# Talking-heads attention and two gated layers on one core: values fetched before the relayouts, fewer clock-keeping matmuls, chunk rows 12 partitions apart, q in its own pool

## The chip, the cores and the metric

The kernel runs on one NeuronCore of a Trainium2 chip. The metric is the device time of one execution in microseconds (us); lower is better. The engines are TensorE (PE, with its weight loads listed as PEld), VectorE (DVE), ScalarE (ACT), GpSimd (POOL) and SyncE (SP). SP, POOL and ACT also issue DMAs; a row of the trace that names such an issue writes the engine as SPq or ACTq.

## The reference

Twelve heads of attention for two batches of 448 positions, with the heads mixed by a 12x12 matrix before the softmax and by another after it, and then two gated layers:

```python
scores = scale * np.matmul(q, k.transpose(0, 1, 3, 2))
scores = np.einsum('bhij,hg->bgij', scores, w_pre)
scores = scores - np.max(scores, axis=-1, keepdims=True)
attn = np.exp(scores)
attn = attn / (np.sum(attn, axis=-1, keepdims=True) + 1e-09)
attn = np.einsum('bhij,hg->bgij', attn, w_post)
out = np.matmul(attn, v)
x = out.transpose(0, 2, 1, 3).reshape(B * S, H * D)          # 896 x 768
x = (silu(x @ w_gate) * (x @ w_val)) @ w_out                 # hidden 1536
y = ((h := x @ w_in) * clip(h + 3, 0, 6) / 6) @ w_out2       # hidden 2048
```

The matrices of the two layers arrive in 64-bit floating point and are turned into pairs of 32-bit parts on the chip.

## The kernel before, in words

**Tiles and chunks.** The 448 query positions of a batch are cut into four tiles (TILES, L34), eight tiles in all, numbered t = 0 to 7. A tile is cut into chunks of ten query rows (KI): the eight tiles have 10, 12, 12, 11, 12, 12, 11 and 10 chunks, 90 in all. Two chunks make a pair, and the main loop takes one pair per step, i = 0 to 44, with two lead-in steps before.

**Scores.** `scores(t, c)` (L152) multiplies q by k for head pair c into two PSUM banks, and `scores_out` (L175) copies them, one head on DVE and one on ACT, into the tile's score buffer S: query rows on the partitions, 13 slots of 448 on the free axis (12 heads and a zero slot). There are two score buffers (L136), so tile t+2 overwrites what tile t held.

**Relayouts.** The mix over heads needs the heads on partitions. `relayout(m)` (L184) takes the ten query rows of chunk m out of S. In the kernel before they stand `ncc` partitions apart (ncc is the tile's number of chunks: 10, 11 or 12). SP sends the first eight rows (8 x 13 slots) to partitions 0 to 103 of a tile sx, and `relayout_rest` (L199) sends the other two rows from POOL to partitions 104 to 127; this POOL transfer is called the rest below. sx holds a pair and has six buffers.

**One step.** In program order step i holds: the exponentials of pair i+1 on ACT; the product of attention and values, `av` (L283) and `av_rest` (L305), of an earlier tile; `postmix(i)` (L253), the mix after the softmax; the softmax weights of pair i+1 on DVE; the copy of the mixed weights; `premix(i+2)` (L208), which reads sx, and its row maxima on DVE; and the scores of a later tile. Attention times values begins in step 5; it needs four pieces of v, which `load_v(0, 0)` to `load_v(0, 3)` fetch in steps 0 to 3. The last piece is read by `av_rest` alone, just ahead of `postmix(5)`.

**Queues.** The order is written out by hand: extra work is hung on steps with `at_step`, at named places within a step, and each engine works its list in order. So does SP, which issues nearly all transfers: q, k, v, the relayouts and the weights of the layers. S is read by the relayouts of a tile until the last of them has landed; only then may the scores of the tile after next be copied into that buffer.

**Clock.** `keep_clock` (L489) issues matmuls on a tile of zeros whose result nobody reads: 7 at the start and 17 after the scores of the first two tiles, ahead of the first premix.

**The layers.** After step 44 come the last products with values, then the two gated layers with their weights streamed in (L411).

Of the kernel before, what the change touches and what calls it, by code (L numbers as in the profile page):

```python
# [7 lines left out]
F32 = mybir.dt.float32  # L8
# [15 lines left out]
KG = 5  # L24
KI = 2 * KG
# [8 lines left out]
TILES = [  # L34
    [(0, 100, 10), (100, 120, 12), (220, 120, 12), (340, 108, 11)],
    [(0, 120, 12), (120, 120, 12), (240, 110, 11), (350, 98, 10)],
]
SQ = 45 * KI

WARM = (7, 17)  # L40

LOOK = 2

# [4 lines left out]
def kernel(  # L48
# [14 lines left out]
    nc = tc.nc  # L63
# [20 lines left out]
    big = ctx.enter_context(tc.tile_pool(name="big", bufs=4, side="right"))  # L84
# [9 lines left out]

    qs, ks, vs = {}, {}, {}

    def new_qk(b):
        qs[b] = big.tile([128, HP * SQ], F32, name=f"q{b}", tag="big")
        ks[b] = big.tile([128, HP, S], F32, name=f"k{b}", tag="big")

    def load_q(b, i0, i1):
        lo, hi = (HP * KI * sum(c for _, _, c in TILES[b][:i]) for i in (i0, i1))
        nc.sync.dma_start(out=qs[b][:, lo:hi], in_=qT[b, :, lo:hi])

    def load_k(b, c0, c1, eng=nc.sync):
# [10 lines left out]
    def load_q0(c0, c1, eng):
        n = TILES[0][0][2] * KI
        eng.dma_start(out=qs[0][:, c0 * n : c1 * n], in_=qT[0, :, c0 * n : c1 * n])

    new_qk(0)  # L120
    load_q0(0, 2, nc.sync)
# [9 lines left out]
    nc.scalar.dma_start(out=W1, in_=w_pre)  # L131
    nc.scalar.dma_start(out=W2.rearrange("p g k -> p (g k)"), in_=w_post)
    nc.gpsimd.tensor_scalar(W1, W1, 0.125, 1.0, ALU.mult, ALU.mult)
    load_q(0, 1, 2)

    Ss = [psc.tile([128, H + 1, S], F32, name=f"S{i}") for i in range(2)]  # L136
    for x in Ss:
# [12 lines left out]
    stiles, pqk = {}, {}  # L150

    def scores(t, c, tags=("pqk", "pqk")):  # L152

        b, i = divmod(t, 4)
        n = TILES[b][i][2] * KI
        if c == 0:
            stiles[t] = Ss[t % 2]
        base = HP * KI * sum(x for _, _, x in TILES[b][:i]) + c * n
        p = [bank(f"pqk{t}_{c}_{e}", tags[e]) for e in range(2)]
        for s in range(2):  # L160
            lo, hi = 64 * s, min(64 * s + 64, n)
            for e in range(2):
                r = slice(64 * e, 64 * e + 64)
                nc.tensor.matmul(  # L164
                    p[e][lo:hi, :S],
                    lhsT=qs[b][r, base + lo : base + hi],
                    rhs=ks[b][r, c, :],
                    start=True,
                    stop=True,
                    tile_position=(64 * e, 64 * s),  # L170
                )
        for e in range(2):
            pqk[t, 2 * c + e] = p[e]

    def scores_out(t, c):  # L175
        n = TILES[t // 4][t % 4][2] * KI
        for e in range(2):
            h = 2 * c + e
            copy = nc.scalar.copy if e else nc.vector.tensor_copy
            copy(stiles[t][:n, h, :], pqk.pop((t, h))[:n, :S])  # L180

    sx = {}

    def relayout(m):  # L184

        t, c = chunks[m]  # L190
        b, i = divmod(t, 4)
        ncc = TILES[b][i][2]
        i, r = divmod(m, 2)
        if r == 0:
            sx[i] = psx.tile([128, 2, S], F32, name=f"sx{i}", tag="sx")
        rows = stiles[t][c : ncc * KI : ncc, :, :]
        nc.sync.dma_start(out=sx[i][0:104, r, :], in_=rows[:8, :, :])

    def relayout_rest(m):  # L199
        t, c = chunks[m]  # L200
        b, i = divmod(t, 4)
        ncc = TILES[b][i][2]
        rows = stiles[t][c : ncc * KI : ncc, :, :]
        nc.gpsimd.dma_start(out=sx[m // 2][104:128, m % 2, :], in_=rows[8:, :H, :])  # L204

    pre, tot, ew, wns, post, ats = {}, {}, {}, {}, {}, {}

# [281 lines left out]
    def keep_clock(n):  # L489

        p = ps.tile([128, 512], F32, name=f"clock{n}", tag="ppost", bufs=BUFS["ppost"])
        for _ in range(n):
            nc.tensor.matmul(p[:, :480], lhsT=idle[:, :128], rhs=idle, start=True, stop=True)

    keep_clock(WARM[0])
    placed = 0
    for t in range(2):
        for c in range(HP):
            scores(t, c, (("pqk", "pqk"), ("ppre", "ppre"), ("ppost", "ppost"), ("ppre", "pav"))[(6 * t + c) % 4])
            scores_out(t, c)  # L500
        if t == 0:
            load_q(0, 2, 3)
            for _ in range(8):
                relayout(placed)
                relayout_rest(placed)
                placed += 1
    keep_clock(WARM[1])
    rests = placed
    new_v(0)


    extra = {i: {"qk0": [], "S0": [], "av2": [], "out2": [], "qk": [], "av": [], "S": [], "rest0": [], "rest1": [], "out": [], "end": []} for i in range(-LOOK, NP)}
# [1 line left out]
    def at_step(i, f, *args, place="end"):  # L514
        extra[i][place].append((f, args))
# [272 lines left out]
```

## Time and profile before

| | us |
|---|---|
| median of 3 runs | 702.42 (701.99 to 703.91) |
| the profiled execution, its own time | 702.33 |
| its span in the trace | 700.5 |
| PE busy in the span | 678.0 (97%) |
| DVE busy | 504.3 (72%) |
| ACT busy | 297.6 (42%) |

The profile page gives busy time, 40 slices of the span and the chain of work that ended last. Its span runs from the first to the last instruction; the execution's own time is 1.83 us longer. A matmul that waits inside its pipeline counts as busy, so 97% is not 97% of the peak.

### The profile page before, as it was taken

How to read it: one execution, taken by the hardware profiler on the slowest of the kernel's cores; microseconds unless marked ns; L12 is line 12 of the kernel's file. 1: busy time of each engine (PE TensorE's matmuls, PEld its weight loads, DVE VectorE, ACT ScalarE, POOL GpSimd, SP SyncE). 2: the span in 40 equal slices, each digit the busy share in tenths (PEclk: the TensorE clock that was granted, in tenths of full speed). 3: DMA queues.
4: the chain of work that ended last, by engine and by line, in shares of the span. 5: the costliest groups of instructions: out<-in, count | busy, mean ns of one | idle time of the engine just before them, and what ended most of it. 6: DMA issues, size and time to landing. Idle time of an engine off the chain costs nothing.

```text
span 700.5 us, 16097 instructions
## 1 busy us (share of the span) xinstructions
PE 678.0 (97%) x6696; PEld 567.5 (81%) x6696; DVE 504.3 (72%) x836; ACT 297.6 (42%) x603; POOL 147.9 (21%) x179
## 2 busy tenths in 40 slices
PE   9769998999899999999999999999999999999998
PEld 3336565666589999999999999999999999999997
DVE  4447779988718888888888656668888888665550
ACT  4435676777623433334333323334455444332320
POOL 2413234542601112111211000004323422000000
PEclk9978999999999999999999999999999999999999
DMA  5574676555502433333324332232233223444420
GB/s 180 176 216 133 174 201 201 165 144 142 162 3 90 134 97 130 95 133 117 109 91 131 112 119 91 94 131 91 90 99 127 91 83 121 146 148 147 144 66 26
DMA packets 34200, 86.69 MB, mean 124 GB/s; under 512 B 9328, under 2 KB 22016, under 8 KB 34128
## 3 DMA queue, kind: packets, MB, share of 16 engines
q1 hardware_dynamic: 26208, 81.01, 36.3%
q0 software_dynamic: 7200, 3.94, 2.4%
q8 instruction: 52, 0.85, 0.5%
q10 hardware_dynamic: 720, 0.73, 0.3%
q14 instruction: 20, 0.16, 0.1%
HBM read 62.20 MB, written 2.75 MB: 93 GB/s over the span
## 4 chain that ended last, share of the span: by engine, by line
PE 87%; DMA 4%; DVE 4%; issue 2%; ACT 2%; SPq 1%; POOL 0%; ACTq 0%; POOLq 0%
PE pi L411 17%; PE pp L411 17%; PE po L411 12%; PE pv L411 11%; PE pg L411 11%; PE ppre L215 4%; PE pqk L164 4%; PE pav L291 4%; PE ppost L261 3%; DMA sx<-S 3%; PE p L411 2%; PE pav L311 2%; DMA v<-in_v_dram 2%; ACT e L236 1%; DVE nm L228 1%
## 5 line engine op out<-in xcount | busy, mean ns | idle before, releaser
L411 PE MATMUL pp<-g,hp 128*128 128x448 f32 x384 | 109.1, 365 | 0.0
L411 PE MATMUL po<-u,ho 128*128 128x448 f32 x288 | 81.7, 364 | 0.0
L652 POOL TENSOR_TENSOR g<-rl,g 128x448 fp32r<-128x448 f32 x32 | 41.7, 1323 | 169.1 <-ACT g L651 169.1
L411 PEld LDWEIGHTS pp<-g,hp 128*128 128x128 f32 x384 | 71.9, 187 | 5.8
L204 POOL DMA_DIRECT2D sx<-S x90 | 52.1, 579 | 105.3 <-issue 25.9
L236 ACT ACTIVATE e<-ppre,nm 128x448 f32<-128x448 f32 x90 | 56.3, 631 | 39.0 <-DVE nm L228 38.9
L411 PE MATMUL pi<-x2h,li 128*128 128x448 f32 x192 | 70.2, 366 | 0.0
L411 PE MATMUL pi<-x2l,hi 128*128 128x448 f32 x192 | 70.0, 364 | 0.0
L411 PE MATMUL pi<-x2h,hi 128*128 128x448 f32 x192 | 69.9, 364 | 0.0
L411 PE MATMUL pp<-g,lp 128*128 128x448 f32 x192 | 69.3, 361 | 0.0
L652 POOL TENSOR_TENSOR u<-sg,u 128x448 fp32r<-128x448 f32 x24 | 32.7, 1382 | 154.1 <-ACT u L651 154.1
L291 PEld LDWEIGHTS pav<-at,v 128*64 128x64 f32 x576 | 28.6, 138 | 36.3 <-ACT xs L334 18.3
L228 DVE TENSOR_REDUCE nm<-ppre 128x1 f32<-128x448 f32 x90 | 51.9, 617 | 7.2 <-PE ppre L215 4.9
L411 PEld LDWEIGHTS po<-u,ho 128*128 128x128 f32 x288 | 54.1, 188 | 3.8
L215 PE MATMUL ppre<-sx,W 64*64 64x448 f32 x360 | 52.9, 555 | 3.2 <-DMA sx<-S 2.8
L261 PE MATMUL ppost<-wn,e 60*64 60x60 f32 x2520 | 53.5, 224 | 1.3 <-issue 0.6
L411 PE MATMUL po<-u,lo 128*128 128x448 f32 x144 | 52.3, 363 | 0.0
L261 PEld LDWEIGHTS ppost<-wn,e 60*64 60x64 f32 x2520 | 47.0, 137 | 4.8 <-ACT at L279 1.7
L164 PE MATMUL pqk<-k,q 64*64 64x448 f32 (+3 forms) x384 | 50.7, 567 | 0.0
L411 PE MATMUL pg<-xl,hg 128*128 128x448 f32 x132 | 48.3, 366 | 0.0
L411 PE MATMUL pv<-xl,hv 128*128 128x448 f32 x132 | 48.3, 366 | 0.0
L411 PE MATMUL pg<-xh,hg 128*128 128x448 f32 x132 | 48.2, 365 | 0.0
(97 smaller groups left out, 1401.4 us busy)
## 6 DMA issues: line engine op xcount, KB each, us to landing
sx<-S SPq DMA_DIRECT2D x90, 182.0 KB
ri<-in_moe_w_in_dram SPq DMA_DIRECT2D x16, 768.0 KB
ro<-in_moe_w_out_dram SPq DMA_DIRECT2D x12, 768.0 KB
rg<-in_moe_w_gate_dram SPq DMA_DIRECT2D x11, 768.0 KB
rv<-in_moe_w_val_dram SPq DMA_DIRECT2D x11, 768.0 KB
rp<-in_moe_w_out_dram SPq DMA_DIRECT2D x12, 640.0 KB
rp<-in_moe_w_out_dram SPq DMA_DIRECT2D x6, 768.0 KB
sx<-S POOLq DMA_DIRECT2D x90, 42.0 KB, 5.4
```

Of the source, the lines that this page charges most:

```text
L164: nc.tensor.matmul(p[e][lo:hi, :S], lhsT=qs[b][r, base + lo : base + hi], rhs=ks[b][r, c, :], start=True, stop=True, tile_position=(64 * e ...
L204: nc.gpsimd.dma_start(out=sx[m // 2][104:128, m % 2, :], in_=rows[8:, :H, :])
L215: nc.tensor.matmul(p[a][64 * r : 64 * r + 64, :S], lhsT=W1[rows, :], rhs=x[rows, r, :], start=True, stop=True, tile_position=(64 * a, 64 * r),
L228: nc.vector.tensor_reduce(nm[:, a : a + 1], pre[i][a][:, :S], AX.X, ALU.max, negate=True)
L236: nc.scalar.activation(e2[a], p[a][:, :S], AF.Exp, bias=nm[:, a : a + 1], scale=1.0, accum_out=sm[:, a : a + 1])
L261: nc.tensor.matmul(p[s][64 * c : 64 * c + 64, at, :, :], lhsT=e2[a][rows, 64 * k : 64 * k + 64], rhs=wn[rows, a, :].rearrange("p (g k) -> ...
L291: nc.tensor.matmul(p[64 * e : 64 * e + 64, : 2 * n], lhsT=vs[b][:, jc, h, :], rhs=ats[t][:, 2 * jc : 2 * jc + 2, h, :n], start=jc == 0, st ...
L311: mm = nc.tensor.matmul(pavs[t, c][64 * e : 64 * e + 64, a * n : a * n + n], lhsT=vs[b][rows, JC - 1, h, :], rhs=ats[t][rows, KB - 1, h, : ...
L411: nc.tensor.matmul(p[:, :S], lhsT=wt[:, kk, :], rhs=xx, start=start, stop=stop)
L652: eng.tensor_tensor(to[1], src, to[0].bitcast(F32), ALU.subtract)
```

## The change

It does five things.

1. q no longer lies in one big buffer per batch. Each tile has its own q tile in a rotating pool of three buffers, and a batch's `big` buffers now hold k alone.
2. The rows of a chunk in S are always 12 partitions apart (STRIDE), whatever the tile's number of chunks. The tiles with 10 and 11 chunks get padding rows in q, so their score buffers fill 118 or 119 partitions where they filled 100 or 110.
3. The first two pieces of v are loaded ahead of the first relayouts; the q of tile 2 goes to SP behind the first eight relayouts.
4. The second run of clock-keeping matmuls has 6 for 17.
5. One early group of scores, (2, 3) in step 4, uses the bank `pav` for one of its two results, where it used `pqk` for both.

```diff
-SQ = 45 * KI
+STRIDE = 12
+ROWS = [[STRIDE * (KI - 1) + n for _, _, n in t] for t in TILES]
-WARM = (7, 17)
+WARM = (7, 6)
...
+    pq = left.enter_context(tc.tile_pool(name="pq", bufs=3, side="left"))
...
-    def new_qk(b):
-        qs[b] = big.tile([128, HP * SQ], F32, name=f"q{b}", tag="big")
+    def new_k(b):
         ks[b] = big.tile([128, HP, S], F32, name=f"k{b}", tag="big")
-    def load_q(b, i0, i1):
-        lo, hi = (HP * KI * sum(c for _, _, c in TILES[b][:i]) for i in (i0, i1))
-        nc.sync.dma_start(out=qs[b][:, lo:hi], in_=qT[b, :, lo:hi])
+    def load_q(t, c0=0, c1=HP, eng=nc.sync):
+        b, i = divmod(t, 4)
+        n = ROWS[b][i]
+        if c0 == 0:
+            qs[t] = pq.tile([128, HP * STRIDE * KI], F32, name=f"q{t}", tag="q")
+        base = HP * sum(ROWS[b][:i])
+        eng.dma_start(out=qs[t][:, c0 * n : c1 * n], in_=qT[b, :, base + c0 * n : base + c1 * n])
...
-    load_q(0, 1, 2)
+    load_q(1)
+    new_v(0)
+    for j in range(2):
+        load_v(0, j)
...
-        n = TILES[b][i][2] * KI
+        n = ROWS[b][i]
...
-        rows = stiles[t][c : ncc * KI : ncc, :, :]
-        nc.sync.dma_start(out=sx[i][0:104, r, :], in_=rows[:8, :, :])
+        rows = stiles[t][c : c + 7 * STRIDE + 1 : STRIDE, :, :]
+        nc.sync.dma_start(out=sx[i][0:104, r, :], in_=rows)
...
-        rows = stiles[t][c : ncc * KI : ncc, :, :]
-        nc.gpsimd.dma_start(out=sx[m // 2][104:128, m % 2, :], in_=rows[8:, :H, :])
+        rows = stiles[t][c + 8 * STRIDE : c + 9 * STRIDE + 1 : STRIDE, :H, :]
+        nc.gpsimd.dma_start(out=sx[m // 2][104:128, m % 2, :], in_=rows)
...
         if t == 0:
-            load_q(0, 2, 3)
             for _ in range(8):
                 relayout(placed)
                 relayout_rest(placed)
                 placed += 1
     keep_clock(WARM[1])
+    load_q(2)
     rests = placed
-    new_v(0)
...
             if t == 2 and c == 3:
-                at_step(4, scores, t, c, place="qk0")
+                at_step(4, scores, t, c, ("pav", "pqk"), place="qk0")
...
-    loads = [(j, load_v, 0, j) for j in (0, 1, 2, 3)] + [(2, load_q, 0, 3, 4), (5, load_q, 1, 0, 1)]
+    loads = [(j - 2, load_v, 0, j) for j in (2, 3)] + [(2, load_q, 3), (5, load_q, 4)]
-    loads += [(13, load_q, 1, 1, 2), (19, load_q, 1, 2, 3), (25, load_q, 1, 3, 4)]
+    loads += [(13, load_q, 5), (19, load_q, 6), (25, load_q, 7)]
...
-                    perm[c + ncc * kk] = s0 + min(kk // KG * KG * ncc + c * KG + kk % KG, n - 1)
+                    perm[c + STRIDE * kk] = s0 + min(kk // KG * KG * ncc + c * KG + kk % KG, n - 1)
```

On SP, before, this is the list from the q of tile 1 to the last piece of v. Each row is an issue or a run of equal ones; sx0 is the first pair of chunks, S0 and S1 are the two score buffers, and 128x768 is one piece of v:

```order
L103 DMA q0_91<-in_q_dram 128x720 x2
L197 DMA sx0_173<-S0_107 104x1x448 x2
L197 DMA sx3_188<-S0_107 104x1x448 x2
L197 DMA sx4_269<-S0_107 104x1x448 x2
L197 DMA sx6_294<-S1_108 104x1x448 x2
L112 DMA v0_259<-in_v_dram 128x768
L197 DMA sx7_350<-S1_108 104x1x448 x2
L112 DMA v0_259<-in_v_dram 128x768
L197 DMA sx8_413<-S1_108 104x1x448 x2
L112 DMA v0_259<-in_v_dram 128x768
L197 DMA sx9_477<-S1_108 104x1x448 x2
L112 DMA v0_259<-in_v_dram 128x768
```

And now, from the same place to the same place (the pairs sx1, sx2 and sx5 are left out of both; the q of tile 3 stands behind sx8 in both):

```order
L108 DMA q1_109<-in_q_dram 128x720
L117 DMA v0_111<-in_v_dram 128x768 x2
L199 DMA sx0_179<-S0_114 104x1x448 x2
L199 DMA sx3_194<-S0_114 104x1x448 x2
L108 DMA q2_254<-in_q_dram 128x720
L199 DMA sx4_265<-S0_114 104x1x448 x2
L199 DMA sx6_290<-S1_115 104x1x448 x2
L117 DMA v0_111<-in_v_dram 128x768
L199 DMA sx7_346<-S1_115 104x1x448 x2
L117 DMA v0_111<-in_v_dram 128x768
L199 DMA sx8_409<-S1_115 104x1x448 x2
```

Two pieces of v moved ahead of all relayouts, the other two moved up to stand behind the 14th and the 16th relayout (before: the last stood behind the 20th), and the q of tile 2 moved down behind the eighth.

On PE, before, in step 4 and at the head of step 5 (pqk2_3 are the scores of tile 2, head pair 3; pav0_0 is the first product with values; the brackets name the semaphores a matmul waits for):

```order
L164 MATMUL pqk2_3_0_578<-k0_92,q0_91 64x448 [waits Activation_49]
L164 MATMUL pqk2_3_1_579<-k0_92,q0_91 64x448 [waits DVE_49]
L215 MATMUL ppre6_0_593<-sx6_294,W1_101 64x448 [waits DMAHW0_49]
L164 MATMUL pqk2_4_0_602<-k0_92,q0_91 64x448 [waits Activation_49]
L291 MATMUL pav0_0_617<-at0_337,v0_259 64x100 [waits DMAHW2_49]
L291 MATMUL pav0_0_617<-at0_337,v0_259 64x100 [waits DMAHW5_49]
L291 MATMUL pav0_0_617<-at0_337,v0_259 64x100 [waits DMAHW0_49]
L311 MATMUL pav0_0_617<-at0_337,v0_259 64x50 [waits DMAHW4_49]
```

And now:

```order
L168 MATMUL pqk2_3_0_573<-k0_94,q2_254 64x448
L168 MATMUL pqk2_3_1_574<-k0_94,q2_254 64x448 [waits Activation_49]
L215 MATMUL ppre6_0_588<-sx6_290,W1_104 64x448 [waits DMAHW2_49]
L168 MATMUL pqk2_4_0_597<-k0_94,q2_254 64x448 [waits DVE_49]
L291 MATMUL pav0_0_611<-at0_333,v0_111 64x100 [waits DVE_49]
L291 MATMUL pav0_0_611<-at0_333,v0_111 64x100 [waits DMAHW4_49]
L311 MATMUL pav0_0_611<-at0_333,v0_111 64x50 [waits DMAHW7_49]
```

The product with values waited for four transfers and now waits for two; the first result of the scores (2, 3) waits for nothing.

## Rows read from the trace of the kernel before

**Rows 1.** The page: span and busy time of PE.
```profile
span 700.5 us, 16097 instructions
...
PE 678.0 (97%) x6696; PEld 567.5 (81%) x6696; DVE 504.3 (72%) x836; ACT 297.6 (42%) x603; POOL 147.9 (21%) x179
```

**Rows 2.** Stages: from:to, length, busy (count) of PE PEld DVE ACT POOL, clock, DMA, GB/s.
```profile
58.00:102.00 44.00, 42.34 (x1180) 27.31 (x1180) 35.53 (x102) 31.04 (x90) 14.88 (x26) 1.00 0.65 180
...
208.00:700.50 492.50, 489.05 (x2417) 452.80 (x2416) 359.87 (x433) 178.99 (x274) 74.36 (x56) 1.00 0.33 109
```

**Rows 3.** Timeline of PE: start, length, line, operation, output<-inputs, count [idle before <-releaser].
```profile
14.56 3.61 PE L493 MATMUL clock<-idle 128*128 128x480 bf16 x17
...
32.15 0.96 PE L215 MATMUL ppre<-sx,W 64*64 64x448 f32 x2 [1.75 <-DMA sx<-S]
...
44.19 0.56 PE L291 MATMUL pav<-at,v 128*64 128x100 f32 x8
47.26 0.39 PE L291 MATMUL pav<-at,v 128*64 128x100 f32 x4 [2.50 <-DMA v<-in_v_dram]
52.09 0.35 PE L311 MATMUL pav<-at,v 64*64 64x50 f32 x2 [4.44 <-DMA v<-in_v_dram]
...
58.11 0.28 PE L261 MATMUL ppost<-wn,e 60*64 60x60 f32 x2
...
59.08 0.97 PE L215 MATMUL ppre<-sx,W 64*64 64x448 f32 x8
...
61.41 0.28 PE L261 MATMUL ppost<-wn,e 60*64 60x60 f32 x2
```

**Rows 4.** Timeline of SP's queue: issues of the first relayouts and of the last piece of v.
```profile
10.96 19.76 SPq L197 DMA_DIRECT2D sx<-S  x14
...
40.45 0.47 SPq L112 DMA_DIRECT2D v<-in_v_dram  x1
```

**Rows 5.** DMA issues up to 60 us: count, KB each, median us from issue to landing.
```profile
sx<-S SPq DMA_DIRECT2D x25, 182.0 KB
...
sx<-S POOLq DMA_DIRECT2D x24, 42.0 KB, 5.4
```

**Rows 6.** Stretches as in rows 2: first loads; tile 0; mixed; tiles 2, 5, 6.
```profile
4.00:8.00 4.00, 4.00 (x29) 1.46 (x32) 1.32 (x3) 2.38 (x4) 0.52 (x2) 1.00 1.06 372
12.00:31.00 19.00, 16.80 (x255) 7.71 (x247) 10.10 (x24) 7.30 (x19) 8.45 (x15) 1.00 0.51 149
32.00:52.00 20.00, 12.52 (x178) 5.92 (x178) 9.49 (x23) 9.04 (x24) 3.44 (x6) 0.81 0.81 219
59.00:63.00 4.00, 4.00 (x120) 2.49 (x113) 3.51 (x12) 2.89 (x9) 2.73 (x6) 1.00 0.57 195
126.00:131.00 5.00, 5.00 (x127) 2.89 (x121) 4.74 (x13) 3.64 (x11) 3.41 (x6) 1.00 0.55 169
147.00:155.00 8.00, 8.00 (x227) 5.26 (x227) 7.18 (x21) 6.42 (x19) 4.86 (x9) 1.00 0.54 140
```

**Rows 7.** Stretches as in rows 2, for the granted clock.
```profile
34.00:37.00 3.00, 3.00 (x46) 1.51 (x42) 2.71 (x7) 1.03 (x5) 1.14 (x2) 0.50 0.82 228
48.00:58.00 10.00, 5.91 (x92) 3.52 (x92) 2.99 (x8) 1.50 (x4) 0.00 (x0) 0.50 0.35 105
```

**Rows 8.** Timeline of POOL: the rest of the tenth relayout.
```profile
22.57 0.58 POOL L204 DMA_DIRECT2D sx<-S  x1 [0.50 <-issue]
```

**Rows 9.** Groups of DVE by shape: busy us, mean ns | idle before, releasers.
```profile
L180 DVE COPY S<-pqk 120x448 f32<-120x448 f32 x24 | 14.9, 619 | 5.6 <-DMA sx<-S 4.4 <-PE pqk L164 0.4
...
L180 DVE COPY S<-pqk 100x448 f32<-100x448 f32 x12 | 7.4, 620 | 5.9 <-PE pqk L164 5.4
```

**Rows 10.** Timeline: first score copies of tiles 4 and 5 on DVE; a premix of tile 7.
```profile
81.11 0.61 DVE L180 COPY S<-pqk 120x448 f32<-120x448 f32 x1
105.40 0.62 DVE L180 COPY S<-pqk 120x448 f32<-120x448 f32 x1 [1.53 <-DMA sx<-S]
171.91 2.02 PE L215 MATMUL ppre<-sx,W 64*64 64x448 f32 x7
```

More of the change, by code (lines that the diff above doesn't have):

```diff
@@ L114, in load_v @@
         )
[L116 to L121, printed above, removed]
+    new_k(0)
+    load_q(0, 0, 2)
     load_k(0, 0, 1, nc.scalar)
     load_k(0, 1, 2)
-    load_q0(2, 6, nc.scalar)
+    load_q(0, 2, 6, nc.scalar)
     load_k(0, 2, 3)
@@ L154, in scores @@
         b, i = divmod(t, 4)
-        n = TILES[b][i][2] * KI
+        n = ROWS[b][i]
         if c == 0:
             stiles[t] = Ss[t % 2]
-        base = HP * KI * sum(x for _, _, x in TILES[b][:i]) + c * n
+        base = c * n
         p = [bank(f"pqk{t}_{c}_{e}", tags[e]) for e in range(2)]
@@ L165, in scores @@
                     p[e][lo:hi, :S],
-                    lhsT=qs[b][r, base + lo : base + hi],
+                    lhsT=qs[t][r, base + lo : base + hi],
                     rhs=ks[b][r, c, :],
@@ L175, in scores_out @@
     def scores_out(t, c):
-        n = TILES[t // 4][t % 4][2] * KI
+        n = ROWS[t // 4][t % 4]
         for e in range(2):
@@ L190, in relayout @@
         t, c = chunks[m]
-        b, i = divmod(t, 4)
-        ncc = TILES[b][i][2]
         i, r = divmod(m, 2)
@@ L195, in relayout @@
             sx[i] = psx.tile([128, 2, S], F32, name=f"sx{i}", tag="sx")
-        rows = stiles[t][c : ncc * KI : ncc, :, :]
-        nc.sync.dma_start(out=sx[i][0:104, r, :], in_=rows[:8, :, :])
+        rows = stiles[t][c : c + 7 * STRIDE + 1 : STRIDE, :, :]
+        nc.sync.dma_start(out=sx[i][0:104, r, :], in_=rows)
     def relayout_rest(m):
         t, c = chunks[m]
-        b, i = divmod(t, 4)
-        ncc = TILES[b][i][2]
-        rows = stiles[t][c : ncc * KI : ncc, :, :]
-        nc.gpsimd.dma_start(out=sx[m // 2][104:128, m % 2, :], in_=rows[8:, :H, :])
+        rows = stiles[t][c + 8 * STRIDE : c + 9 * STRIDE + 1 : STRIDE, :H, :]
+        nc.gpsimd.dma_start(out=sx[m // 2][104:128, m % 2, :], in_=rows)
     pre, tot, ew, wns, post, ats = {}, {}, {}, {}, {}, {}
@@ L560 @@
                 at_step(i + part // step, x_split, t, part)
-    at_step(4, new_qk, 1)
+    at_step(4, new_k, 1)
     at_step(13, new_v, 1)
@@ L742 @@
         part = []
-        for s0, n, ncc in TILES[b]:
-            perm = np.zeros(ncc * KI, int)
+        for (s0, n, ncc), rows in zip(TILES[b], ROWS[b]):
+            perm = np.zeros(rows, int)
             for c in range(ncc):
                 for kk in range(KI):
-                    perm[c + ncc * kk] = s0 + min(kk // KG * KG * ncc + c * KG + kk % KG, n - 1)
+                    perm[c + STRIDE * kk] = s0 + min(kk // KG * KG * ncc + c * KG + kk % KG, n - 1)
             part.append(by_pairs(q[b : b + 1, :, perm, :]).reshape(128, HP * len(perm)))
```

## The prediction

> **What bounds the kernel now.** I read the page first, then the stages, then PE's timeline of the stages where PE is idle, and last the DMA rates there. The page gives PE 678.0 of 700.5 us [rows 1]: 22.5 us at most can come from PE never waiting, and more only from matmuls that run at a lower clock. The last stage, from 208 us on, is PE at 489.05 of 492.5 us [rows 2]; nothing of the change touches it, so it only slides. What can be won lies before it, and mostly before 58 us.
>
> There PE's timeline shows a relay of transfers [rows 3]. The tenth relayout, the last of tile 0, gates a premix at 32.15 (PE idle 1.75). The first product with values begins at 44.19, waits 2.50 for v and again 4.44, and its last part starts at 52.09. That wait belongs to the last piece of v, issued at 40.45 [rows 4] behind twenty relayouts. [...] So the postmix of step 5 (right behind the 52.09 row) and that of step 6 (58.11) stand 6.0 us apart, while the next stands 3.3 behind (61.41) [rows 3].
>
> Why the transfers are late: a relayout with its rest is 182 + 42 KB [rows 5], 229,376 B. While tile 0 (rows 10 apart) is sent, the DMAs move 149 GB/s, for tile 6 (11 apart) 140, for tiles 2 and 5 (12 apart) 195 and 169 [rows 6]. Those stretches hold almost nothing but relayouts. So a relayout with rows 12 apart costs 1.18 to 1.36 us; I take 1.27. Tile 0's ten took from 12 us, where data starts to flow behind the first issue at 10.96 [rows 4], to 32.15 [rows 3]: 20.15 us, 2.0 each.
>
> **The change, part by part.**
>
> *Rows 12 apart, tile 0.* Ten relayouts at 1.27 are 12.7 us. The q of tile 2 now stands between the eighth and the ninth: 368,640 B at 219 GB/s, the rate while loads and relayouts are mixed [rows 6], is 1.7. The tenth has landed at 12 + 12.7 + 1.7 = 26.4 instead of 32.15. Bounds: at 1.18 each 25.5; with no help from the distance 12 + 20.15 + 1.7 = 33.85; and if POOL's rest keeps its old pace (the tenth issued at 22.57 [rows 8], 5.4 to landing [rows 5]) 28.0. [...]
>
> *Values first.* The two pieces of v ahead of the relayouts (128 x 768 values of 4 bytes each) are 786,432 B, less the 368,640 B of q that leave this place: 417,792 B, 1.1 us at the 372 GB/s of the first loads [rows 6]. The queues are nearly empty just before 12 us, so this lies beside the copies of tile 0's scores: nothing. If it did not fit, it delays the first relayout by that 1.1. Behind the tenth relayout there are then six relayouts and two pieces of v up to the last one: 2.16 MB, 9.9 us at 219 GB/s, landing at 36.3.
>
> *When PE gets there.* From the gate of the tenth relayout to the first product with values PE took 44.19 - 32.15 = 12.0 us, and the product itself 0.56 + 0.39 [rows 3]. I keep that whole: 26.4 + 12.0 + 0.95 = 39.4, later than v at 36.3, so v is hidden by 3 us. The end of the row at 52.09 moves to 39.4: **-12.7**. (The 3 us at half clock inside those 12.0 [rows 7] could give back up to 1.5; I count none, since a wait of the same kind remains.) If v's cover goes, PE waits for it microsecond by microsecond.
>
> *The half clock of step 5.* With no long wait before it, step 5 takes 3.3 and not 6.0: **-2.7**. Bounds 0 and -2.7.
>
> *What is late next.* PE now runs 15.4 us earlier, the transfers must follow. Tile 4's first score copy (81.11 [rows 10], now 65.7) needs all of tile 2's relayouts landed. From the tenth to the thirty-fourth relayout there are 24 relayouts, two pieces of v, two loads of q (128 x 714 and 128 x 720) and four of k (128 x 448): 7.94 MB. At 219 GB/s they have landed at 62.7, at the 180 of the next stage [rows 2] at 70.5; that is a stall of 0 to 4.8. I take about 195, the rate of rows 12 apart: 67.1, **+1.5** rounded.
>
> *Tile 3, 11 apart to 12.* The first score copy of tile 5 waits 1.53 for tile 3's relayouts at 105.40 [rows 10], and PE loses about 1.0 by it; with rows 12 apart the eleven relayouts save some 0.3 each (229,376 B at 140 against 169 GB/s), 3 in all: **-1.0** (0 to -1.6).
>
> *Tile 7, 10 apart to 12.* Seven premix matmuls take 2.02 at 171.91 [rows 10] where eight take 0.97 [rows 3], waiting inside for a relayout: **-1.0** (0 to -1.5). Around it DVE sets the pace, so no more.
>
> *Edits at nothing.* Copies of 118 or 119 partitions for 100 or 110: 620 against 619 ns [rows 9]. Padding in q: the first tile's is 55,296 B, 0.15 us at 372 GB/s. The scores in `pav`: one wait less in step 4, before a gate that comes later; the product with values now waits for that bank's copy, half a step older. The 11 matmuls gone are 11 x 3.61/17 = 2.3 us [rows 3]; PE ends them at 15.8 instead of 18.2, and the first premix must wait for the second relayout, at about 12 + 2.5 + 1: their loss gains nothing by itself and only uncovers a wait. The q pool's third buffer: tile 3's q follows tile 0's, read long before.
>
> **Sum:** -12.7 - 2.7 + 1.5 - 1.0 - 1.0 = -15.9. Against the profiled execution's own 702.33 us (span 700.5 and 1.83 around it; the median of the runs shown, 702.42, is 0.09 above): **686.4**.
>
> **The rivals.**
>
> *Only the order pays.* The distance between rows does nothing and the rates differ for other reasons (rests, queue depth). Then the tenth relayout lands at 33.85, v at 43.7, the row at 52.09 moves to 46.8 (-5.3), the half clock goes (-2.7), the transfers behind cost 1.5: 695.8. For it: each rate is of one stretch. Against: all four stretches sort themselves by distance. 0.13.
>
> *The transfers take it back.* PE is early, but the DMAs move only 180 GB/s all the way: stall 4.8 at tile 4, and about 0.5 more later: 690. For: the queues are hardly idle from 12 to 52 us. 0.15.
>
> *The clock never falls.* The 1.5 above comes too, relayouts cost 1.18 (-0.9) and tile 4 does not stall (-1.5): 682.5. 0.09.
>
> *Slower: the clock falls at the start and stays down.* [...] If all seven steps 0 to 6 ran so, +18.9 against -15.9: 705.3; it decides from six such steps on. For: both half-clock stretches followed waits of 1.75 us and more. Against: from 12 to 31 us PE is idle for 2.2 of 19.0 us, and the clock there is 1.00 [rows 6]. [...] 0.04.
>
> *It does not do what it says:* the premixes wait for rests or q at the old pace, and nothing moves: 702. 0.03.
>
> **How the numbers follow.** The forecast itself has 0.56. Its time is 686.4. Low end: the unfallen clock with half of its chance below, 681. High end: the first rival's time nearly, 695; about half of it and the last two cases lie outside. That leaves out less than 2 in 10. Faster by over 0.3% (2.1 us, about what a measurement of this kernel tells from no change): 0.56 + 0.13 + 0.15 + 0.09 = 0.93. Same 0.03, slower 0.04.
>
> **What would show it.** Right: the gate of the tenth relayout near 26 us; no wait of PE for v over 1 us; the granted clock 1.00 through step 5; the postmix of step 6 at about 42.7 for 58.11; 165 to 200 GB/s while tile 0 is sent; no wait of the score copies for transfers at tile 5. Wrong: a rate of 150 GB/s for tile 0, a long wait of the score copies of tile 3 or 4 for relayouts, or a half clock between 15 and 40 us.

## The result and the profile after

The changed kernel takes 694.1 us (median of 693.01, 693.97, 694.22 and 695.58); its ratio to the kernel before is 0.9876, interval 0.9849 to 0.9902. Faster, as forecast, and inside the range of 681 to 695, 0.9 us under its upper end; but the forecast was 686.4, so some 9 us came of the 16 that were foreseen. The profiled execution took 693.01 us, its span 691.2, 9.3 less than the 700.5 before.

The page answers to [rows 1]: PE is now busy for 98% of the span.
```profile
span 691.2 us, 16079 instructions
...
PE 674.4 (98%) x6685; PEld 565.7 (82%) x6685; DVE 505.6 (73%) x836; ACT 297.0 (43%) x603; POOL 147.7 (21%) x179
```

The stretches of the changed kernel, with the columns of rows 2, answer to [rows 2, 6, 7]:
```profile
10.00:12.00 2.00, 2.00 (x24) 0.85 (x20) 1.27 (x3) 1.09 (x3) 0.96 (x2) 1.00 0.20 75
12.00:31.00 19.00, 17.49 (x316) 8.46 (x310) 12.76 (x32) 10.38 (x27) 9.02 (x16) 1.00 0.67 205
32.00:52.00 20.00, 16.80 (x413) 10.57 (x409) 14.56 (x40) 11.58 (x33) 6.12 (x11) 1.00 0.71 205
34.00:37.00 3.00, 1.31 (x23) 0.42 (x13) 2.35 (x7) 1.90 (x6) 1.14 (x2) 1.00 0.67 194
48.00:58.00 10.00, 9.83 (x272) 6.19 (x263) 8.74 (x25) 6.93 (x21) 2.29 (x4) 1.00 0.70 201
76.00:79.00 3.00, 0.91 (x18) 0.13 (x9) 1.47 (x4) 1.46 (x5) 0.00 (x0) 1.00 0.92 245
79.00:84.00 5.00, 4.94 (x90) 3.40 (x94) 2.29 (x6) 1.15 (x3) 3.32 (x6) 0.66 0.72 225
500.00:520.00 20.00, 20.00 (x98) 18.17 (x97) 17.66 (x18) 7.84 (x14) 7.81 (x6) 1.00 0.25 82
```

Tile 0 is sent at 205 GB/s where it was 149, the clock is 1.00 from 34 to 37 and from 48 to 58 us where it was 0.50. New is the stretch at 76 to 79 us: PE works for 0.91 of 3 us, and behind it the clock falls, to a mean of 0.66. PE's timeline, answering to [rows 3]:
```profile
14.47 1.39 PE L493 MATMUL clock<-idle 128*128 128x480 bf16 x6
...
26.84 0.93 PE L215 MATMUL ppre<-sx,W 64*64 64x448 f32 x4
...
37.52 0.72 PE L215 MATMUL ppre<-sx,W 64*64 64x448 f32 x4 [2.21 <-issue]
...
39.30 0.74 PE L291 MATMUL pav<-at,v 128*64 128x100 f32 x12
39.96 0.26 PE L311 MATMUL pav<-at,v 64*64 64x50 f32 x2
39.98 0.28 PE L261 MATMUL ppost<-wn,e 60*64 60x60 f32 x2
...
43.27 0.26 PE L261 MATMUL ppost<-wn,e 60*64 60x60 f32 x1
...
79.06 0.59 PE L215 MATMUL ppre<-sx,W 64*64 64x448 f32 x2 [2.15 <-issue]
...
181.09 0.28 PE L261 MATMUL ppost<-wn,e 60*64 60x60 f32 x2
```

The product with values runs its twelve parts without a wait; the postmix of step 6 stands at 43.27 for 58.11. An issue wait, as in [2.21 <-issue], is idle time of PE for which the profile shows nobody who ended it. Up to step 6 the kernel is 14.84 us ahead. At the postmix of step 44 (181.09) it is 11.29 ahead, at the end 9.3. The row of before for step 44, and its stretch in the layers:
```profile
192.38 0.28 PE L261 MATMUL ppost<-wn,e 60*64 60x60 f32 x2
...
507.00:527.00 20.00, 20.00 (x101) 18.55 (x100) 17.06 (x20) 10.50 (x18) 5.26 (x5) 1.00 0.35 116
```

So two questions are left: where 3.55 us went between steps 6 and 44, and where 2.0 went in the layers, which the change does not touch.

### The profile page after: what moved, and what is told of

Same layout as the page of the kernel before. It is cut to its first block, busy times and chain, and to the rows that moved or that the text cites. A ratio compares the mean times of both kernels' runs of the same rounds, so it can differ in the third digit from the quotient of the medians.

```text
span 691.2 us, 16079 instructions
## 1 busy us (share of the span) xinstructions
PE 674.4 (98%) x6685; PEld 565.7 (82%) x6685; DVE 505.6 (73%) x836; ACT 297.0 (43%) x603; POOL 147.7 (21%) x179
## 3 DMA queue, kind: packets, MB, share of 16 engines
q1 hardware_dynamic: 26208, 81.14, 36.3%
## 4 chain that ended last, share of the span: by engine, by line
PE 89%; DVE 5%; ACT 2%; issue 2%; POOL 1%; DMA 1%; ACTq 0%; POOLq 0%
PE pi L411 17%; PE pp L411 17%; PE po L411 13%; PE pg L411 12%; PE pv L411 12%; PE pqk L168 4%; PE pav L291 4%; PE ppre L215 4%; PE ppost L261 4%; PE p L411 2%; ACT e L236 2%; PE pav L311 2%; DVE nm L228 2%; DVE wn L248 1%; DVE at L279 1%
## 5 line engine op out<-in xcount | busy, mean ns | idle before, releaser
L215 PE MATMUL ppre<-sx,W 64*64 64x448 f32 x360 | 50.7, 544 | 5.2 <-issue 4.4
L168 PE MATMUL pqk<-k,q 64*64 64x448 f32 (+3 forms) x384 | 48.3, 546 | 1.0 <-issue 0.7
L411 PE MATMUL pv<-xh,lv 128*128 128x448 f32 x132 | 48.2, 365 | 0.0
```

Of the source, the lines that this page charges most:

```text
L168: nc.tensor.matmul(p[e][lo:hi, :S], lhsT=qs[t][r, base + lo : base + hi], rhs=ks[b][r, c, :], start=True, stop=True, tile_position=(64 * e ...
L215: nc.tensor.matmul(p[a][64 * r : 64 * r + 64, :S], lhsT=W1[rows, :], rhs=x[rows, r, :], start=True, stop=True, tile_position=(64 * a, 64 * r),
L411: nc.tensor.matmul(p[:, :S], lhsT=wt[:, kk, :], rhs=xx, start=start, stop=stop)
```

## The experiments

Three numbers of each profile carry the comparison: the start of the postmix of step 6, the time from there to the postmix of step 44, and from there to the end of the span. The ratios are to the kernel before on the same chip. Chips and executions differ by a few us, so the intervals are about as wide as the effects behind step 6, and the traces have to do the telling. The kernel before took 703.2 us in the comparison of the result (median of four), 706.0 on the chip of e1 to e4, and 703.2 to 704.0 on the others; so a time of e1 to e4 is held against a forecast in us by its ratio, times 703.2. Postmix(i) is the start of the postmix of step i.

| run | postmix(6) at | to postmix(44) | to the end | ratio, interval |
|---|---|---|---|---|
| before | 58.11 | 134.27 | 508.1 | |
| before_again | 56.94 | 133.33 | 508.1 | |
| the change | 43.27 | 137.82 | 510.1 | 0.9876, 0.9849 to 0.9902 |
| after_again | 44.08 | 140.08 | 510.1 | 0.9868, 0.9821 to 0.9915 |
| e1_rows | 47.09 | 139.46 | 510.4 | 0.9921, 0.9885 to 0.9957 |
| e2_order | 55.04 | 136.01 | 513.6 | 0.9978, 0.9950 to 1.0006 |
| e3_warm | 45.94 | 137.24 | 510.1 | 0.9901, 0.9866 to 0.9936 |
| e4_v1late | 41.50 | 142.54 | 513.6 | 0.9890, 0.9856 to 0.9924 |
| e5_extra | 43.60 | 138.72 | 513.8 | 0.9963, 0.9931 to 0.9996 |
| e6_spread | 42.45 | 138.93 | 513.5 | 0.9882, 0.9840 to 0.9924 |
| e7_vahead | 42.26 | 136.62 | 513.4 | 0.9863, 0.9832 to 0.9893 |
| e7_again | 42.72 | 134.69 | 510.2 | 0.9826, 0.9787 to 0.9866 |
| e8_vboth | 42.28 | 139.90 | 510.1 | 0.9865, 0.9825 to 0.9906 |
| e9_gaps | 43.48 | 134.95 | 513.4 | 0.9860, 0.9814 to 0.9906 |

### One part undone at a time

**e1_rows**, the old distance:
```diff
-ROWS = [[STRIDE * (KI - 1) + n for _, _, n in t] for t in TILES]
+ROWS = [[KI * n for _, _, n in t] for t in TILES]
...
-        rows = stiles[t][c : c + 7 * STRIDE + 1 : STRIDE, :, :]
+        rows = stiles[t][c : c + 7 * n + 1 : n, :, :]
...
```


> Undoes the distance alone: rows of a chunk 10, 11 or 12 apart as before, all else as in the change. Forecast's account (the transfers of tile 0 run at the rate of their distance): tile 0 goes at about 149 GB/s again instead of 205, its tenth relayout lands some 5 us later than 26.6, the first premixes wait again, and postmix(6) comes at 46 to 48 instead of 43.3; 697 to 699 us. Rival (the distance is worth nothing, the rate rose because other transfers stand between the relayouts): the rate stays near 200 GB/s and the time within 1.5 us of 694.1. A second rival, that PE's instruction fetch gives back what comes early: postmix(6) late by 3 to 5 us, but the idle of 2.15 us ahead of premix(17) shrinks, 695 to 697.

**e2_order**, the old order of q and v:
```diff
-    new_v(0)
-    for j in range(2):
-        load_v(0, j)
...
+            load_q(2)
             for _ in range(8):
...
-    loads = [(j - 2, load_v, 0, j) for j in (2, 3)] + [(2, load_q, 3), (5, load_q, 4)]
+    loads = [(j, load_v, 0, j) for j in (0, 1, 2, 3)] + [(2, load_q, 3), (5, load_q, 4)]
```


> Undoes the order alone: q of tiles 1 and 2 ahead of the first relayouts and v's four pieces in steps 0 to 3, rows 12 apart and 6 clock-keeping matmuls kept. Forecast's account: relayouts land as fast as in the change, but v's last piece lands behind 16 more relayouts; PE waits 5 to 8 us for v at tile 0's value products, its clock falls to half in the step behind, postmix(6) at 52 to 56; 700 to 704 us. Rival (the faster relayouts alone bring it, v is there in time): within 2 us of 694.1.

Tile 0's stretch and PE's waits, of e1_rows and then of e2_order:
```profile
12.00:31.00 19.00, 15.18 (x186) 6.52 (x182) 9.98 (x24) 7.16 (x19) 8.24 (x15) 0.89 0.54 155
...
28.94 1.07 PE L217 MATMUL ppre<-sx,W 64*64 64x448 f32 x6 [2.02 <-DMA sx<-S]
```
```profile
12.00:31.00 19.00, 17.29 (x258) 8.01 (x251) 11.47 (x29) 9.38 (x25) 8.80 (x16) 0.91 0.60 184
...
45.35 0.60 PE L288 MATMUL pav<-at,v 128*64 128x100 f32 x4 [4.94 <-DMA v<-in_v_dram]
49.64 0.35 PE L308 MATMUL pav<-at,v 64*64 64x50 f32 x2 [3.69 <-DMA v<-in_v_dram]
```
With the order equal, the distance alone is 155 against 205 GB/s; with the old order it is 149 against 184. All fourteen profiles sort themselves so: 184 to 207 GB/s in the eleven with rows 12 apart, where the tenth relayout landed at 26.5 to 28.8 us, and 149 to 155 in the three with the old rows, where it landed at 31.5 to 32.1. So the rows 12 apart do speed the relayouts, and a premix waits for transfers again without them. But the order weighs more: postmix(6) goes from 58.11 to 47.09 with the order and without the distance, to 55.04 with the distance and without the order, and to 43.27 with both, since without the order v is late (4.94 and 3.69) however fast the relayouts go. The other three parts of the change are in all three; the q pool and the bank `pav` were never undone by themselves, and what they bring is not told apart. Both came out as the forecast's account had it, in us a little above its upper ends (699.45 and 704.1), by their ratios inside (697.6 and 701.6).

**e3_warm**, 17 clock-keeping matmuls again:
```diff
-WARM = (7, 6)
+WARM = (7, 17)
```


> Undoes the clock-keeping matmuls alone: 17 for 6. Forecast's account (they lie in a wait and cost nothing): within 0.7 us of 694.1. Rival: premix(0) in the change starts at 15.79, right behind the sixth, so eleven more at 0.20 us hold it up by 2.2 us; some 1.3 us of that is taken back from waits up to 28 us; 695 to 696.5. If the waits that the trace calls issue, at 35.3, follow the instruction fetch and not PE, they take in the rest: 694 to 695.

```profile
14.04 3.62 PE L493 MATMUL clock<-idle 128*128 128x480 bf16 x17
20.07 0.97 PE L215 MATMUL ppre<-sx,W 64*64 64x448 f32 x4 [0.74 <-ACT e L236]
21.40 0.81 PE L261 MATMUL ppost<-wn,e 60*64 60x60 f32 x40 [0.37 <-DVE wn L248]
```
The first postmix stands at 21.40, in the change at 19.61, in its second profile at 21.35. So the eleven matmuls cost PE nothing that the change does not lose in another execution. The time, 696.28, lies inside the rival's 695 to 696.5; its interval overlaps the change's and separates neither.

### One program, executed again

**after_again** and **before_again** are the two kernels unchanged.

> The changed kernel itself once more, for what differs between two executions of one program. If the waits that the trace calls issue (in the change 2.2 us at 35.3, 0.8 at 43.7, 2.2 at 76.9, 0.7 at 119.9) are set by the program alone, they stand at the same steps within 0.3 us; if PE's instruction fetch meets the transfers by chance, the relayouts up to postmix(6) come within 1 us of the same times but the issue waits stand at other steps, each ending 1.3 to 1.7 us after a packet of the instruction queue has landed. From postmix(44) to the end: 510.1 again if the 207 ns spacing of the layer's products between 450 and 600 us belongs to the program, 508 or 513.5 if it belongs to the execution. Ratio to the kernel before 0.985 to 0.991.

> The kernel before once more. The waits that the prediction rests on (ppre for the tenth relayout near 32 us, pav for v up to 52 us, the half clock behind it) come back within 1 us, since they follow the transfers' order; the short issue waits at 80.8 and 86.6 move to other steps if they are chance, stay if they are the program's; from postmix(44) to the end 508.2 again if the spacing of the layer's products is the program's.

Of after_again: two stretches, PE's wait for v, one score copy on DVE, and PE's issue waits:
```profile
19.00:24.00 5.00, 4.89 (x72) 2.42 (x70) 2.78 (x9) 3.03 (x9) 2.44 (x5) 0.66 0.74 214
...
507.00:527.00 20.00, 20.00 (x98) 18.16 (x98) 17.05 (x20) 10.82 (x18) 6.08 (x5) 1.00 0.35 119
...
40.77 0.26 PE L311 MATMUL pav<-at,v 64*64 64x50 f32 x2 [1.16 <-DMA v<-in_v_dram]
...
49.67 0.62 DVE L184 COPY S<-pqk 119x448 f32<-119x448 f32 x1 [2.08 <-DMA sx<-S]
...
76.64 0.62 PE L261 MATMUL ppost<-wn,e 60*64 60x60 f32 x26 [1.19 <-issue]
91.91 0.39 PE L261 MATMUL ppost<-wn,e 60*64 60x60 f32 x11 [0.53 <-issue]
```
Of before_again:
```profile
31.56 0.96 PE L215 MATMUL ppre<-sx,W 64*64 64x448 f32 x2 [1.20 <-DMA sx<-S]
47.06 0.60 PE L291 MATMUL pav<-at,v 128*64 128x100 f32 x4 [3.82 <-DMA v<-in_v_dram]
51.45 0.35 PE L311 MATMUL pav<-at,v 64*64 64x50 f32 x2 [3.79 <-DMA v<-in_v_dram]
...
507.00:527.00 20.00, 20.00 (x100) 18.55 (x99) 17.78 (x20) 10.09 (x18) 7.40 (x6) 1.00 0.36 119
```
Of before_again, what the prediction rests on returns within 1.2 us: the gate at 31.56, v at 51.45. The slow step behind v returns too, 5.48 us from postmix(5) to postmix(6) (51.46 to 56.94); the half clock from 34 to 37 us does not: 56 postmix matmuls take 1.32 us at 34.54, where 52 took 2.12 at 35.58 in before. The issue waits of the change do not: they move from 37.5, 44.5, 79.1 and 120.6 us to 76.6 and 91.9. In after_again, where none of them has held PE up before step 7, another wait stands: at 49.67 DVE has waited 2.08 us until tile 1's relayouts have left the score buffer that tile 3's first scores are to fill, and from postmix(6) to postmix(9) it takes 13.68 us, where the change's first profile took 11.48. And v is not hidden here: without an issue wait ahead of it, PE waits 1.16 us for the last piece at 40.77. The granted clock was down near 20 us, to a mean of 0.66 from 19 to 24.

### Does the issue wait come from PE's instructions, and these from the transfers?

A DMA queue that the page calls instruction, q8, moves 16 KB at a time: 52 packets and 0.85 MB in the changed kernel, one to 129 of PE's 6685 matmuls. I take it for the one that carries PE's instructions. One such packet is in the stretch in which PE stands still (DMA queues from 76.2 to 77.4 us: packets, MB, share of 16 engines):
```profile
...
q8 instruction: 1, 0.02, 6.0%
```
It landed at 77.39, and PE went on at 79.06. In the fourteen profiles of this study PE has 37 issue waits of 0.4 us or more between 13 and 200 us, and all 37 end 1.32 to 1.67 us after such a packet landed, while the packets come some 4 to 5 us apart. At that spacing about 3 of 37 would fall there by chance. Their places say the same: counted in PE's matmuls from the start of the program, all 37 stand, to within one, on a grid of 127 matmuls (number 470, 597, 724 and so on), in every kernel. In e3_warm, which has eleven matmuls more in front, the wait at number 470 comes eleven matmuls earlier in the work, inside a postmix and not in the premix behind it. So the place goes by the count of instructions and not by what the step waits for, and I read these waits as waits for instructions. There is one such wait in the two profiles of before and 36 in the twelve others. The packets ahead of a wait took 0.9 to 1.4 us, as the others did; what is late, by this reading, is their start. What makes it late was tried in three ways.

**e4_v1late**:
```diff
-    loads += [(14 + 2 * j, load_v, 1, j) for j in range(JC)]
+    loads += [(20 + 2 * j, load_v, 1, j) for j in range(JC)]
```


> The change with the four pieces of the second batch's v asked for in steps 20 to 26 instead of 14 to 20, nothing else. Theory A (the idle of 2.15 us ahead of premix(17) at 76.9 is PE's instruction fetch, late behind the transfers queued there, and the half clock of the step behind follows from it): the idle falls under 0.8 us, the clock stays at 1.00 from 79 to 86, postmix(17) comes 3 to 4.5 us earlier; 689.5 to 691.5 us, unless a fetch is late in the steps that now carry v. Theory B (the idle is a wait for the chunk's data, or something that PE's own order sets): the idle stays at 1.5 us or more, within 1 us of 694.1.

**e5_extra**:
```diff
+    def load_more(j):
+        nc.sync.dma_start(out=xtra[:, j, :], in_=kT[0, :, j * S : (j + 1) * S])
...
+    loads = [(23, load_more, j) for j in range(4)] + [(j - 2, load_v, 0, j) for j in (2, 3)] + ...
```


> The change with four more loads (four pieces of k, 224 KB each, into a tile that nothing reads) on SP's queue at step 23, where the change shows no issue wait longer than 0.1 us between 85 and 119 us. Theory A (a fetch of PE's instructions is late behind transfers): some 4 us of added transfers bring an issue wait of 0.8 to 2.5 us within the 12 us behind the loads' issue, ending 1.3 to 1.7 us after an instruction packet; 695 to 698 us. Theory B (issue waits have nothing to do with the transfers): no issue wait there; PE either waits for no one or for the relayouts of tile 4 by name; 694 to 695.

**e6_spread**:
```diff
-    ... (5, load_q, 4)]
+    ... (8, load_q, 4)]
-    loads += [(13, load_q, 5), (19, load_q, 6), (25, load_q, 7)]
-    loads += [(14 + 2 * j, load_v, 1, j) for j in range(JC)]
-    loads += [(n, fetch, 0, "early") for n in (12, 14, 16)] + ...
+    loads += [(15, load_q, 5), (19, load_q, 6), (25, load_q, 7)]
+    loads += [(20 + 2 * j, load_v, 1, j) for j in range(JC)]
+    loads += [(n, fetch, 0, "early") for n in (11, 13, 15)] + ...
```


> The change with loads spread away from where relayouts go: v of the second batch in steps 20 to 26 for 14 to 20, q of tile 4 in step 8 for 5, of tile 5 in step 15 for 13, the first weight a step earlier. Theory A: fewer issue waits in steps 5 to 20, under 2 us in sum against 5.7 in the change (35.3, 43.7, 48.6 and 76.9), no half clock; 688 to 692 us. Theory B: the sum of issue waits stays above 4 us; 692 to 697.

Of e4_v1late: the stretch that held the long wait, tile 3's first score copy and PE's issue waits. Of e5_extra and e6_spread one wait each:
```profile
74.00:86.00 12.00, 12.00 (x302) 7.43 (x296) 10.36 (x28) 8.35 (x24) 5.67 (x10) 1.00 0.68 203
...
48.30 0.62 DVE L184 COPY S<-pqk 119x448 f32<-119x448 f32 x1 [3.27 <-DMA sx<-S]
...
46.89 0.46 PE L261 MATMUL ppost<-wn,e 60*64 60x60 f32 x17 [1.09 <-issue]
...
55.64 0.53 PE L168 MATMUL pqk<-k,q 64*55 64x448 f32 x1 [1.53 <-issue]
```
```profile
115.95 0.51 PE L262 MATMUL ppost<-wn,e 60*64 60x60 f32 x20 [0.69 <-issue]
...
208.84 0.47 PE L412 MATMUL pg<-xh,hg 128*128 128x448 f32 x1 [3.10 <-ACT hg L401]
```
```profile
48.38 0.62 DVE L184 COPY S<-pqk 119x448 f32<-119x448 f32 x1 [2.40 <-DMA sx<-S]
...
79.54 0.59 PE L215 MATMUL ppre<-sx,W 64*64 64x448 f32 x2 [1.00 <-issue]
```
In e4_v1late PE never stops from 74 to 86 us and the clock stays, as theory A wanted; but waits of 1.09 and 1.53 stand in steps 7 and 8, which the edit does not reach, and the time (697.03, by its ratio 695.4) misses theory A's forecast and does not settle theory B's. e6_spread has 1.00 left at 79.5, and that is all in steps 5 to 20, under 2 as theory A wanted; but the unedited kernel has 1.7 there in its second profile, the clock falls all the same (0.50 from 50.5 to 53.5 us), and the time (696.98) is no better. In e5_extra the added loads are followed by a wait of 0.69, less than the 0.8 foreseen; its time is of no use, because a weight of the layers came late too (3.10 at 208.84), in this profile alone. So that transfers make instructions late fits, and is not shown.

### The transfers as the next bound

**e7_vahead**, all of v ahead of the relayouts, where the queues were nearly empty (75 GB/s from 10 to 12 us):
```diff
-    for j in range(2):
+    for j in range(JC):
         load_v(0, j)
...
-    loads = [(j - 2, load_v, 0, j) for j in (2, 3)] + [(2, load_q, 3), (5, load_q, 4)]
+    loads = [(2, load_q, 3), (5, load_q, 4)]
```


> The change with all four pieces of v asked for ahead of the first relayout, where the DMA engines moved 75 GB/s between 10 and 12 us, instead of two there and two in steps 0 and 1. Theory A (from step 5 to step 9 the transfers are the bound: some 8 MB of q, v and 22 relayouts have to land before tile 3's first scores can be copied, at 205 to 218 GB/s, and the pieces of v in between cost 3.7 us of that): no wait of DVE or ACT for relayouts at S in steps 6 to 9 and none of PE for v, postmix(9) at 51 to 54 us against 54.75 to 57.76 in the change's two profiles; 688 to 692 us. Rival (what is lost behind step 5 is PE's instruction fetch alone): postmix(5) and postmix(9) keep their times within 1 us; 693 to 696.

**e7_again** is the same kernel.

> e7_vahead once more. If the spacing of the products belongs to the program, both stretches stand at 206.7 ns again and from postmix(44) to the end it takes 513.4 to 513.6 us; if it belongs to the execution, one stretch or both stand at 202.7 (508 to 510.2). Up to postmix(5): 38.4 to 39.6 us again, no wait of PE for v. The issue waits move to other steps. Ratio to before 0.983 to 0.990.

**e8_vboth** is e7_vahead with the edit of e4_v1late.

> As e7_vahead, and the second batch's v in steps 20 to 26 for 14 to 20, as in e4_v1late. If loads among the relayouts of steps 14 to 18 make PE's instruction fetch late there (every profile that has them there, of either kernel, shows issue waits of 1.1 to 3.7 us between steps 14 and 18), none over 0.5 us stands there, and steps 14 to 18 take 17.0 to 17.6 us against 18.2 in the change's first profile; 686 to 690 us. If not, the waits stay, 688 to 692.

Of e7_again: the stretch that now carries v, the first score copy of tile 3, a stretch in each layer:
```profile
10.00:12.00 2.00, 2.00 (x27) 0.84 (x20) 1.62 (x4) 1.34 (x4) 0.12 (x1) 1.00 0.96 359
300.00:320.00 20.00, 20.00 (x100) 18.53 (x100) 16.34 (x20) 8.17 (x12) 5.11 (x4) 1.00 0.34 118
500.00:520.00 20.00, 20.00 (x99) 18.16 (x98) 17.05 (x20) 10.82 (x18) 5.83 (x5) 1.00 0.35 119
...
47.31 0.62 DVE L184 COPY S<-pqk 119x448 f32<-119x448 f32 x1 [0.38 <-DMA sx<-S]
```
Of e7_vahead:
```profile
300.00:320.00 20.00, 20.00 (x99) 18.16 (x98) 15.71 (x20) 7.31 (x11) 2.61 (x2) 1.00 0.27 89
500.00:520.00 20.00, 20.00 (x99) 18.16 (x98) 17.88 (x20) 8.75 (x15) 7.80 (x6) 1.00 0.30 104
```
The wait at the score buffer is down to 0.38 us in one profile and gone in the other, postmix(9) stands at 53.19 and 53.77 against 54.75 and 57.76 in the change, and from step 6 to step 44 it takes 136.62 and 134.69 us against 137.82 and 140.08. Up to step 9 e8_vboth and e9_gaps have this order of v too, and after_again, e4_v1late and e5_extra that of the change: postmix(9) is at 53.19, 53.37, 53.77 and 56.05 with v ahead, at 54.75, 55.14, 57.17 and 57.76 without. The 56.05 is e8_vboth's, whose copy waits 2.2 us. So the transfers were a bound there, and the order of v likely takes part of it away, not in every execution. The time of e7_vahead, 694.58, misses its forecast of 688 to 692 nevertheless: its layers took 3.3 us longer than the change's. That of e7_again, 690.57, is inside. e8_vboth does not add to that: 1.55 us of issue wait stand at 75.25, against its expectation, tile 3's copy waits as said, and the time, 694.26, misses both of its forecasts. (Its premise was wrong as well: before has 0.59 us of issue wait in steps 14 to 18, before_again none.) The kernel of e7_vahead and e7_again is the fastest seen, but its better interval, 0.9787 to 0.9866, overlaps the change's; that it is the faster one is likely, and not shown by time.

### The layers

**e9_gaps**, e7_vahead with two short waits on PE:
```diff
+    def gap():
+        mark = nc.gpsimd.memset(act.tile([1, 1], F32, name="turn2", tag="turn2"), 0.0)
+        tc.add_manual_dep(mark.ins, tail[-1], in_turn, reason="a gap on PE")
+        hold.append(mark.ins.name)
...
+        if j == 0 or (kind, idx) == ("i", 0):
+            gap()
```


> e7_vahead with two short waits put on PE: GpSimd sets one number when PE's last product matmul is done, and PE's next matmul waits for it, once ahead of the first product over the second half of the tokens (near 201 us) and once ahead of the first product of the second layer (near 451 us). Theory (the spacing of the products, 202.7 or 206.7 ns, is a state of PE that an idle of PE sets anew: the spacing changed to 202.5 behind the idle of 3.1 us in e5_extra, and stood there in both profiles of before, which idle 0.2 us some 4 us earlier): each wait costs 0.2 to 1 us, the products between 200 and 364 us and between 453 and 571 us run at 202 to 203 ns, and from postmix(44) to the end it takes 508.5 to 510.5 us against 513.45 in e7_vahead; 689 to 692 us. Rival (the spacing has nothing to do with idle): one or both stretches keep 206.7 ns and the waits only cost; 694 to 696.

```profile
194.57 0.47 PE L418 MATMUL p<-xh,hg 128*128 128x448 f32 x1 [0.36 <-POOL turn L408]
...
451.21 0.47 PE L418 MATMUL pi<-x2h,hi 128*128 128x448 f32 x1 [0.27 <-POOL turn L408]
...
300.00:320.00 20.00, 20.00 (x101) 18.53 (x100) 16.05 (x20) 8.04 (x12) 3.32 (x3) 1.00 0.33 118
400.00:420.00 20.00, 20.00 (x100) 18.34 (x99) 12.22 (x16) 5.70 (x8) 0.00 (x0) 1.00 0.36 121
500.00:520.00 20.00, 20.00 (x99) 18.16 (x98) 17.02 (x18) 8.29 (x14) 6.97 (x6) 1.00 0.22 80
```
The waits cost 0.36 and 0.27 us, as meant. Behind the first the products run fast (101 in 20 us at 300 us), behind the second they stay slow (99 at 500 us), and the stretch at 400 us became slower than in any other profile (PEld 18.34 of 20 us, 18.54 in both kernels' first profiles and in e7_again). The theory that an idle of PE sets the spacing to the fast value falls, and the time, 693.65, lies between its forecast and the rival's.

## Why the prediction was right, and where it was not

- **Tile 0's rate and gate: right.** 205 GB/s, better than the 165 to 200 named. The tenth relayout lands at 26.57 for the forecast 26.4 (at 28.80 in the second profile), and its premix starts at 26.84, with no wait for a transfer. With nothing but the distance changed it is 155 against 205 GB/s (e1_rows and the change), a factor of 1.3. Why the distance does it, no run shows.
- **v hidden, -12.7: right in size, by luck in part.** The row at 52.09 is now at 39.96: -12.1. But v was not hidden by 3 us. Its last piece landed, by its semaphore, at 38.95 and not at 36.3, and at 40.73 in the second profile: in the 12.4 us behind the tenth relayout the DMAs moved 2.66 MB (at 215 GB/s), where the sum had 2.16. And the 12.0 us that were kept whole hold other things: from the gate to the product with values it takes 12.46 us with an issue wait of 2.21 inside, which the forecast did not have, and 9.9 in the second profile without one. Without that wait PE would have come to the row at about 37.75, before v; in the second profile it did come before v and waited 1.16 us, over the 1 us that the prediction allowed. PE's way was too long in the forecast and v's too short, each by some 2 us, and the two met.
- **Half clock of step 5, -2.7: right.** Postmix(5) to postmix(6) takes 43.27 - 39.98 = 3.29 at a granted clock of 1.00, where before took 6.0 [rows 3] at 0.50 [rows 7].
- **Transfers late next, +1.5: mis-sized and misplaced.** It stood for all that is given back before the layers, and that is, net, 3.55 us in this profile and 5.8 in the second (140.08 - 134.27; 6.8 against before_again). Tile 4's first copy, where the forecast put it, waits 0.25 us. The transfers hold up the copy one tile earlier, tile 3's in step 7: 0.68 us in the first profile, where the issue wait had already stopped PE, and 2.08 in the second. The prediction had named a long wait of tile 3's or tile 4's copies as a sign against it, and that sign is there. The largest loss of the first profile is PE's own: the idle of 2.15 us at 76.9 and the half clock behind it made step 15 to step 16 take 7.3 us for 3.4. That is more than the net 3.55 by itself, since waits that the kernel before had in other steps are gone.
- **Tile 3, -1.0, and tile 7, -1.0: they came, and did not last.** No copy of tile 5 waits for transfers any more, and seven premix matmuls of tile 7 take 1.07 for 2.02. The lead over the kernel before goes from 11.67 us at step 23 to 13.15 at step 24, where the copy had waited, and is back at 11.85 at step 27, behind an issue wait; it goes from 11.05 at step 38 to 12.07 at step 39, where the premix had waited, and is back at 11.14 at step 40. The 1.53 of the copy was also one execution's: in before_again it waits 0.54.
- **"Nothing of the change touches the layers, so they only slide": wrong, +2.0.** They took 508.1 us in both profiles of before and 510.1 in both of the change. The second layer's first product ran 98 matmuls in 20 us for 100 or 101. That the change does it is not shown: undoing one part (e1 to e3) did not bring the faster spacing back, and e5_extra had it.
- **Sum.** -14.84 + 3.55 + 2.0 = -9.3. The two terms that carried the sum came within 0.6 us, the first of them by two errors that met; the term behind them was too small by 2, two small ones did not last, and one was not thought of. The range held, but its upper end was drawn from a rival that falls, and not from what went wrong.
- **The rivals.** *Only the order pays* falls by e1_rows; yet the order's share was larger than that rival gave it (postmix(6) at 47.09, where its 46.8 for the row ahead of postmix(5) and a step of 3.3 made about 50). *The transfers take it back* came nearest, in the mechanism and in the time, 690, but at another tile. *Slower by the clock* is there at most in small: with 6 matmuls the clock was down near 20 us in 4 of 11 profiles (0.66 from 19 to 24 us in after_again), with 17 in none of 3, and three are too few to put it down to the eleven matmuls. In after_again the first postmix came at 21.35 for 19.61, but in e8_vboth, whose clock stayed up there, at 21.14, so what the clock costs in it is not told apart; it is far from the six steps at which this rival decides.

Open stays whether and why an instruction packet starts late, and what sets the spacing of the products in the layers.

## What to carry to other kernels

When a chain of transfers is shortened, follow the same queue on to the next buffer that must come free: here the gain ended at tile 3's first copy (0.68 and 2.08 us of wait), one tile earlier than the one first looked at. Fill a stretch in which the queues are nearly empty (75 GB/s from 10 to 12 us in the change, 359 in e7_again) with loads that are needed later, before they come to stand among transfers that gate. And before reading a difference of a few us, profile the same program twice: here its parts differed by up to 3.3 us between two executions.

## What the hardware showed that was not expected

- **PE waits for its own instructions, by all signs.** All 37 waits of 0.4 us or more that the trace calls issue end 1.32 to 1.67 us after a 16 KB packet of the instruction queue landed. They take 0.4 to 2.7 us each. Their places are fixed, every 127 matmuls from the start of the program; at which of these places PE waits differs from execution to execution.
- **The same matmuls keep one of several spacings through a whole stage.** The mean distance between starts is 202.7 or 206.7 ns in the first layer's gate and value products, 202.6 or 206.7 in the second layer's first product, with the granted clock at 1.00 in both. e7_vahead and e7_again are one program and differ (513.4 and 510.2 us behind step 44). The second layer's first product was fast only in the two profiles of before and in e5_extra; in e9_gaps the output products of both layers went from 202.2 to 204.4 as well.
